# A gated mix of a long convolution and a token MLP on one core: two copies moved, an activation table loaded elsewhere, accumulating transfers reordered and re-timed in the planner

## The chip, the cores and the metric

The kernel runs on one core of a Trainium2 chip. The metric is the device time of one execution in microseconds. Before the change the median of three runs is 180.29 us (179.93 to 180.88). The profiled execution took 179.5 us; its span, from the first recorded instruction to the last, is 177.7 us, and the times below count from the start of that span. The granted TensorE clock was 1.00 all through.

A core has engines that run side by side, each through its own instruction list in order: TensorE (PE; matmuls, whose weight loads are the row PEld), VectorE (DVE), ScalarE (ACT), GpSimd (POOL) and SyncE (SP), which here issues the loads and stores. [...]

## The reference

With S = 2048 rows and D = 640 columns in bf16, and x = q:

```python
g = sigmoid((x * gate_w).sum(-1, keepdims=True))
# branch a: a 4-tap causal filter on k, times v, then a causal convolution of length S by FFT
kv = shift_filter(k, shift_k) * v
y  = irfft(rfft(pad(kv)) * rfft(pad(ssm_k)))[:S] + kv * ssm_D
a  = q * y
# branch b: layernorm over D, then an MLP over the tokens (S -> 1536 -> S)
h = layernorm(x)
u = gelu(einsum("sd,sf->df", h, w1) + b1)
b = (einsum("df,fs->ds", u, w2) + b2).T
out = g * a + (1 - g) * b
```

## The kernel before

The convolution is computed as matmuls with a table of sines (FTB), in stages. The filter ssm_k is transposed (transp, wT), transformed (fwd_c for its first half, fwd_even and fwd for its second) into C[0] and C[1], and combined across residues by additions on VectorE (mixing). k is filtered by matmuls against KF (kv), multiplied by v, transformed into C[2] (first half of the rows) and C[3] (second half), and combined in the same way. Then the spectra are multiplied on VectorE (cross, product), combined back (invmix) and transformed back by matmuls (inverse). The MLP's two products, m1 (48 groups of 8 matmuls, X with a ring of w1) and m2 (16 output tiles, GT with W2), are independent of it until the outputs are summed in O1. They have the lowest priority and fill TensorE wherever the convolution has nothing ready.

Four PSUM tiles of two banks each are shared: at most two for the MLP, at most three for the convolution. ScalarE empties nearly all of them (act), and a matmul group that finds no free tile waits.

The order of the work on each engine isn't written by hand. Every operation is given to a planner (class _Sched) with its engine, a modelled length, its reads and writes, and a priority (by default its number in the order of the program). SC.run() lets a model clock run: whenever an engine is free, the ready operation with the lowest priority value is taken. The order that comes out is then emitted, with the semaphore waits that the data need, and is fixed from there on. If the model believes a transfer to have landed sooner than it does, the instruction is emitted too early in its list and waits on the chip, with everything behind it.

What the change touches:

- **Transfers in the planner** (lines 459 to 464). All transfers share one model queue, dma_free. A transfer is due when that queue has moved it, plus 2.0 us, and plus another 6.0 if GpSimd issued it.
- **Accumulating transfers** (dma with accum=True, line 267), issued by GpSimd: they add an SBUF region into another one. Four of them form the second half of the filter's spectrum (v1mix, line 1058), two are in mixing_acc (line 1112) for C[3], four in cross (line 1250), one each in the products with a late part (line 1214), four in acc_dma (line 1227), which add the cross terms V1 into A1, and four in inverse for the first half of the output. In mixing_acc the sum and difference of lines 1113 and 1114 need both transfers of line 1112.
- **Key turns** (k_turn, line 760): VectorE reorders a block of k (kn) into kp, then SyncE issues a transposing transfer into KT. Blocks 0 and 1 have priority 0, so they go where the planner believes their data to be there.
- **Row statistics** (stats_of and ln_tile): VectorE computes mean and variance of the 16 row tiles of X in groups of 8, 5 and 3; GpSimd forms the inverse deviation (ln_scale); VectorE applies it (ln_apply). The operations are chained by `after` into one order, statistics of the next group ahead of the applies of the last.
- **Gelu** (line 1138): the first one comes when the first m1 tile is done. The activation table that it needs is loaded by an instruction that stands right ahead of it in ScalarE's list.

An `after` edge in the planner is an order of starts only; it places an operation in the emitted list and adds no wait for data.

Of the kernel before, what the change touches and what calls it, by code (L numbers as in the profile page):

```python
# [328 lines left out]
class _Sched:  # L329
# [59 lines left out]
    def run(self):  # L389
        ops = self.ops  # L390
        for op in ops:
            op.succ = []
            op.asucc = []
            op.ndep = len(op.deps) + len(op.after)
        for op in ops:
            for d in op.deps:
                d.succ.append(op)
            for d in op.after:
                d.asucc.append(op)
        engs = list(ENGS) + ["SP", "QA"]  # L400
        ready = {e: [] for e in engs}
        pend = {e: [] for e in engs}
        free = {"ACT": 2.93, "DVE": 0.85, "POOL": 0.83, "PE": 1.18, "SP": 0.0, "QA": 0.0}
        port = {"DVE": 0.0, "POOL": 0.0}
        dma_free = 0.3
        avail = {}
        for op in ops:
            avail[op] = 0.0
            if op.ndep == 0:
                heapq.heappush(pend[op.eng], (0.0, op.prio, op.idx))  # L410
        nfree = list(range(self.NSLOT))
        held = {}
        events = []
        order = []
        t = 0.0
        done = 0
        started = 0
        n = len(ops)
        frees = []
        while started < n:  # L420
            while frees and frees[0][0] <= t:
                _, sl, cls = heapq.heappop(frees)
                nfree.append(sl)
                held[cls] -= 1
            nxt = []
            progress = False
            for e in engs:
                while pend[e] and pend[e][0][0] <= t:
                    _, p, i = heapq.heappop(pend[e])
                    heapq.heappush(ready[e], (p, i))  # L430
                if free[e] > t:
                    nxt.append(free[e])
                    continue
                skipped = []
                pick = None
                while ready[e]:
                    p, i = heapq.heappop(ready[e])
                    op = ops[i]
                    if op.vt is not None and op.vt.slot is None:
                        c = op.vt.cls  # L440
                        if not nfree or held.get(c, 0) >= self.limit.get(c, 99):
                            skipped.append((p, i))
                            continue
                    pick = op
                    break
                for s in skipped:
                    heapq.heappush(ready[e], s)
                if pick is None:
                    if pend[e]:
                        nxt.append(pend[e][0][0])  # L450
                    continue
                op = pick
                progress = True
                started += 1
                if op.vt is not None and op.vt.slot is None:
                    op.vt.slot = nfree.pop(0)
                    held[op.vt.cls] = held.get(op.vt.cls, 0) + 1
                op.start = t
                if e in ("SP", "QA") or op.lat < 0:
                    issue = 1.2 if e == "POOL" else 0.1  # L460
                    s = max(t + issue, dma_free)
                    dma_free = s + op.dur
                    op.end = dma_free + 2.0 + (6.0 if e == "POOL" else 0.0)
                    free[e] = t + issue
                else:
                    op.end = t + op.dur
                    if op.lock:
                        op.end += max(port["POOL" if e == "DVE" else "DVE"] - t, 0.0)
                        port[e] = op.end
                    free[e] = op.end  # L470
                order.append(op)
                if op.vt is not None:
                    op.vt.left -= 1
                    if op.vt.left == 0:
                        heapq.heappush(frees, (op.end + 0.05, op.vt.slot, op.vt.cls))
                for s in op.asucc:
                    avail[s] = max(avail[s], op.start)
                    s.ndep -= 1
                    if s.ndep == 0:
                        heapq.heappush(pend[s.eng], (avail[s], s.prio, s.idx))  # L480
                for s in op.succ:
                    lat = 0.08 if s.eng == e else 0.15
                    if e == "PE" and s.eng == "PE":
                        lat = 0.0
                    avail[s] = max(avail[s], op.end + lat)
                    s.ndep -= 1
                    if s.ndep == 0:
                        heapq.heappush(pend[s.eng], (avail[s], s.prio, s.idx))
                nxt.append(free[e])
            if not progress:  # L490
                c = [x for x in nxt if x > t]
                if frees:
                    c.append(frees[0][0])
                assert c, "schedule stuck: " + str([(o.name, o.eng, o.ndep) for o in ops if not hasattr(o, "end")][:12])
                t = min(c)
        self.order = order
        self.makespan = max(o.end for o in ops)
        return order
# [16 lines left out]
def _build(nc, A_q, A_k, A_v, A_shift_k, A_ssm_k, A_ssm_D, B_x, B_w1, B_b1, B_w2, B_b2, gate_w, out):  # L515
# [10 lines left out]
    with ExitStack() as es:  # L526
# [434 lines left out]
        def ln_scale(a, b):  # L961
            n = b - a
            ts("POOL", sd[:, a:b], mv[:, a:b, 1], 1e-5, None, ALU.add, prio=0)
            o_ = tt("POOL", rstd[:, a:b], sd[:, a:b], V(cst, 1, [[0, n]]), ALU.pow, prio=0)
            o_.dur, o_.lock = 1.75, False
            tt("POOL", sd[:, a:b], sd[:, a:b], rstd[:, a:b], ALU.mult, prio=SDP)
# [15 lines left out]
        for h in range(2):  # L982
            for db in range(ND):
                transp(h, db)
            if h == 0:
                consts()
            if h in (1,):
                fwd_even(srcW(h), h, C[h], 1.0 / 1024.0, h == 1, "W")
            if h == 0:
# [5 lines left out]
            if h == 0:  # L995
                LB = [0, 8, 13, 16]
                nb = len(LB) - 1
                seq = []

                def chain(f, *a):  # L1000
                    n0 = len(SC.ops)
                    f(*a)
                    for o_ in SC.ops[n0:]:
                        if o_.eng == "DVE":
                            o_.after.update(seq[-1:])
                            seq.append(o_)

                pag = []

                def flush():  # L1010
                    while pag:
                        o_ = pag.pop(0)
                        o_.after.update(seq[-1:])
                        seq.append(o_)

                def stats_of(k):
                    for t in range(LB[k], LB[k + 1]):
                        b0, b1, ag = ln_tile(t // 4, t % 4)
                        b0.after.update(seq[-1:])
                        seq.append(b0)  # L1020
                        flush()
                        b1.after.update(seq[-1:])
                        seq.append(b1)
                        pag.append(ag)
                    ln_scale(LB[k], LB[k + 1])
                stats_of(0)
                for k in range(1, nb):
                    stats_of(k)
                    flush()
                    chain(ln_apply, LB[k - 1], LB[k])  # L1030
                chain(ln_apply, LB[nb - 1], 16)
                lnlast.append(seq[-1])
                for g0 in KFP:
                    tt("POOL", KF[:, g0:g0 + 20 // len(KFP), :, :], V(cw, 7 * g0, [[7, 20 // len(KFP)], [1, 7], [0, 32]]), V(m32, 0, [[0, 20 // len(KFP)], [0, 7], [1, 32]]), ALU.mult).after.update(kfirst[:1])
                    kfirst.append(SC.ops[-1])
                for hk in range(2):
                    k_turn(hk)
                mixing(C[0], SS, 0, fine=True, prio=MIXP)
            else:
                mixing(C[1], C[0], 0, conj=True, prio=MIXP)  # L1040
# [283 lines left out]
        lastp = []  # L1324
        chained(product, A1[1], A1[1], V0[1], tmp_of(q_hi, 0), V1[1])
        chained(product, A1[0], A1[0], V0[0], tmp_of(q_hi, 1), V1[0])
        acc_dma(A1[1], V1[1])
        acc_dma(A1[0], V1[0])
        chained(product, A0[1], A0[1], V0[1], H(V0[1], 0))
        lastacc = SC.ops[-1]  # L1330
        assert lastacc.eng == "POOL"
        for kt in range(2):
            dma(q_hi[:, kt, :, :], dr(A_q, 512 * kt * D, [[4 * D, 128], [1, 4 * D]]), 128 * 5120, wait=[H(A0[1], 1)]).deps.add(lastacc)
# [45 lines left out]
```

## Time and profile before

| Engine | busy us | share of the 177.7 us span |
|---|---|---|
| TensorE | 172.6 | 97% |
| TensorE weight loads | 129.4 | 73% |
| VectorE | 169.7 | 96% |
| ScalarE | 117.0 | 66% |
| GpSimd | 43.6 | 25% |

The share of time in which an engine is busy is an average over the stages. A busy TensorE row says little by itself, since matmuls overlap and their ends are modelled; the number of matmuls in a stretch, times the time of one, tells whether it runs without a break. The transfers' two large queues moved 32.16 MB (those of SyncE) and 11.14 MB (those of GpSimd, the accumulating ones). The table of transfers in the profile gives the time from issue to landing, of which waiting behind other transfers is a part.

### The profile page before, as it was taken

The page shows a single profiled execution, that of the slowest core. Times are in us where ns is not written, and L with a number is a line of the kernel's source. Part 1 is how long each engine was busy: PE and PEld are TensorE (multiplying, and loading weights), DVE is VectorE, ACT ScalarE, POOL GpSimd, SP SyncE. Part 2 cuts the span into 40 slices and gives each one's busy share as a digit, 9 for nine tenths or more (in the row PEclk, how much of TensorE's full clock was granted, in tenths as well). Part 3 has the DMA queues.
Part 4 walks back from the last instruction along what each step waited for, and adds up shares of the span by engine and source line. Part 5 has one row for each costly group of instructions (what it writes and reads, how often), then busy time and mean ns, then how long its engine had stood idle before and what let it go on. Part 6 is the DMA issues. An engine that isn't in the chain of part 4 may idle for free.

```text
span 177.7 us, 3342 instructions
## 1 busy us (share of the span) xinstructions
PE 172.6 (97%) x1380; PEld 129.4 (73%) x1381; DVE 169.7 (96%) x203; ACT 117.0 (66%) x176; POOL 43.6 (25%) x52
## 2 busy tenths in 40 slices
PE   7999999799999999999999999999999999999993
PEld 2666787487788776777777778888888887777772
DVE  7899789989999999999999999999999999999974
ACT  4999997998999999529999911231321323754760
POOL 8089803300000065000241101204343000252000
PEclk9999999999999999999999999999999999999999
DMA  4999999999999999999999998898999999499363
GB/s 136 394 411 374 391 312 156 248 414 374 191 240 315 109 216 226 231 228 278 230 227 271 205 248 299 144 225 230 188 193 217 207 218 408 167 197 212 93 241 131
DMA packets 38542, 43.51 MB, mean 245 GB/s; under 512 B 15867, under 2 KB 31360, under 8 KB 38528
## 3 DMA queue, kind: packets, MB, share of 16 engines
q1 hardware_dynamic: 33296, 32.16, 61.2%
q0 software_dynamic: 5200, 11.14, 36.5%
q8 instruction: 11, 0.18, 0.5%
q14 instruction: 3, 0.02, 0.0%
q10 hardware_dynamic: 32, 0.01, 0.0%
HBM read 25.87 MB, written 2.62 MB: 160 GB/s over the span
## 4 chain that ended last, share of the span: by engine, by line
PE 88%; DMA 5%; ACT 3%; SPq 2%; issue 0%; DVE 0%
PE pp L298 88%; DMA rows<-in_B_b_dram 5%; SPq L272 2%; ACT C L676 1%; ACT L676 1%; ACT GT L676 0%; DVE O L688 0%
## 5 line engine op out<-in xcount | busy, mean ns | idle before, releaser
L298 PE MATMUL pp<-X,ring 128*128 128x320 bf16 x384 | 55.3, 299 | 0.0
L632 DVE TENSOR_TENSOR C<-C 128x2560 bf16<-128x2560 bf16 (+2 forms) x37 | 54.5, 1523 | 0.8 <-ACT C L676 0.6
L298 PE MATMUL pp<-GT,W 128*128 128x320 bf16 x384 | 52.6, 299 | 0.0
L298 PEld LDWEIGHTS pp<-GT,W 128*128 128x128 bf16 x384 | 43.5, 113 | 8.7
L298 PEld LDWEIGHTS pp<-X,ring 128*128 128x128 bf16 x384 | 37.3, 98 | 14.3
L676 ACT ACTIVATE C<-pp 128x640 bf16<-128x640 f32 x64 | 40.7, 731 | 2.8 <-PE pp L298 2.7
L676 ACT ACTIVATE O<-pp,c,omg 128x640 bf16<-128x640 f32 x15 | 13.3, 885 | 34.7 <-PE pp L298 34.7
L267 POOL DMA_DIRECT2D C<-C x8 | 11.0, 1616 | 43.9 <-DVE C L632 43.9
L298 PE MATMUL pp<-wT,FTB 128*128 128x320 bf16 x112 | 17.1, 299 | 0.7 <-ACT GT L676 0.5
L676 ACT ACTIVATE cgb<-pp,gg 128x640 bf16<-128x640 f32 x16 | 12.7, 795 | 5.6 <-PE pp L298 5.2
L676 ACT ACTIVATE GT<-pp,cc 128x640 bf16<-128x640 f32 x12 | 9.6, 803 | 9.3 <-PE pp L298 9.2
L298 PEld LDWEIGHTS pp<-wT,FTB 128*128 128x128 bf16 x112 | 10.5, 98 | 5.6 <-ACT GT L676 0.8
L632 DVE TENSOR_TENSOR tm<-C,C 128x2560 bf16<-128x2560 bf16 (+1 forms) x7 | 14.3, 2059 | 0.0
L954 DVE BATCH_NORM_STATS2 stats<-X 128x6 f32<-128x320 bf16 x32 | 13.6, 464 | 0.5 <-DMA X<-in_A_q_dram 0.5
L298 PE MATMUL pp<-C,FTB 128*128 128x320 bf16 x96 | 13.4, 299 | 0.0
L267 POOL DMA_DIRECT2D C<-q_hi x6 | 5.9, 977 | 27.6 <-DVE C L632 12.9
L298 PEld LDWEIGHTS pp<-C,FTB 128*128 128x128 bf16 x96 | 9.4, 98 | 3.6
L676 ACT ACTIVATE gq<-gq 128x640 bf16<-128x640 bf16 x16 | 11.8, 745 | 0.2 <-DVE gq L632 0.2
L632 DVE TENSOR_TENSOR SS<-C 128x2560 bf16<-128x2560 bf16 x8 | 11.7, 1488 | 0.1
L632 DVE TENSOR_TENSOR C<-tm 128x2560 bf16<-128x2560 bf16 (+1 forms) x9 | 10.7, 1194 | 0.1
L676 ACT ACTIVATE ksh<-pp 128x1024 bf16<-128x1024 f32 (+1 forms) x12 | 9.9, 903 | 0.2 <-PE pp L298 0.2
L267 POOL DMA_DIRECT2D O<-q_hi x4 | 4.8, 1200 | 21.3 <-DVE q_hi L632 21.3
(77 smaller groups left out, 197.0 us busy)
## 6 DMA issues: line engine op xcount, KB each, us to landing
ring<-in_B_w_dram SPq DMA_DIRECT2D x12, 512.0 KB, 12.2
W<-in_B_w_dram SPq DMA_DIRECT2D x12, 512.0 KB, 5.5
C<-C POOLq DMA_DIRECT2D x8, 640.0 KB, 11.5
X<-in_A_q_dram SPq DMA_DIRECT2D x4, 640.0 KB, 8.4
kn<-in_A_k_dram SPq DMA_DIRECT2D x4, 640.0 KB, 9.4
out_dram<-O SPq DMA_DIRECT2D x7, 320.0 KB, 3.4
C<-SS POOLq DMA_DIRECT2D x3, 640.0 KB, 11.9
ssm<-in_A_ssm_k_dram SPq DMA_DIRECT2D x3, 512.0 KB, 6.8
```

Source lines behind the costliest of these rows:

```text
L267: ins = engobj.dma_start(out_ap, in_ap, accum_op=ALU.add, max_dma_last_dim=2560)
L272: ins = engobj.dma_start(out_ap, in_ap)
L298: ins = self.nc.tensor.matmul(ps_ap, lhsT=lhsT, rhs=rhs, start=start, stop=stop, skip_group_check=True)
L632: o_ = SC.add(eng, d, lambda s: T.op(eng, lambda e: e.tensor_tensor(o, a, b, op), rd, [o]), rd, [o], prio=prio, name="tt")
L676: return T.op("ACT", lambda e: e.activation(o, src, func, **kw), rr + [src], ww)
L954: ops.append(SC.add("DVE", 0.38, (lambda o, i: lambda s: T.op("DVE", lambda e: e.bn_stats(o, i), [i], [o]))(o, i), [i], [o]))
```

## The change

Three edits to the order, and one to the planner's model:

1. The two key turns of the first half get an `after` edge to the second statistics instruction of tiles 13 and 15, so they stand between the statistics of the last group.
2. A gelu of one column is put on ScalarE behind the last transposed block of the filter's second half, so that the table is loaded there. Its output, gws, is overwritten later by its real value.
3. The four accumulating transfers of acc_dma for A1 get an `after` edge to the one that belongs to the product A0[1], which so stands ahead of them in GpSimd's list. The query reload that frees q_hi for the outputs waits for that one.
4. In the planner, accumulating transfers leave the shared queue and get one of their own: 0.6 us after their issue, one after the other, 2.2 times their modelled length each, with nothing added. The other transfers are no longer held up by them in the model.

```diff
+        acc_free = 0.0
...
-                    s = max(t + issue, dma_free)
-                    dma_free = s + op.dur
-                    op.end = dma_free + 2.0 + (6.0 if e == "POOL" else 0.0)
+                    if e == "POOL":
+                        acc_free = max(t + issue + 0.6, acc_free) + 2.2 * op.dur
+                        op.end = acc_free
+                    else:
+                        s = max(t + issue, dma_free)
+                        dma_free = s + op.dur
+                        op.end = dma_free + 2.0
...
             if h == 0:
                 consts()
+            else:
+                g_ = act(gws[:, :], cst[:, 1:2], ACT.Gelu_apprx_tanh, name="tab", prio=SC.ops[-1].idx)
+                g_.dur = 1.5
+                g_.after.add(SC.ops[-2])
...
+                kpos = []
...
                         pag.append(ag)
+                        if t in (13, 15):
+                            kpos.append(b1)
...
                     k_turn(hk)
+                    SC.ops[-2].after.add(kpos[hk])
...
+        n_acc = len(SC.ops)
         acc_dma(A1[1], V1[1])
         acc_dma(A1[0], V1[0])
         chained(product, A0[1], A0[1], V0[1], H(V0[1], 0))
         lastacc = SC.ops[-1]
+        for o_ in SC.ops[n_acc:]:
+            if o_.eng == "POOL" and o_ is not lastacc:
+                o_.after.add(lastacc)
```

## The prediction

> **What bounds the kernel now.** I read the busy shares first, then the chain of work that ended last, then the timelines of TensorE and VectorE around the places that the diff names, and last the accumulating transfers one by one.
>
> ```profile
> PE 172.6 (97%) x1380; PEld 129.4 (73%) x1381; DVE 169.7 (96%) x203; ACT 117.0 (66%) x176; POOL 43.6 (25%) x52
> ```
>
> Two engines are nearly full. The chain says which of them sets the end:
>
> ```profile
> 31.60 1.28 ACT L676
> 32.89 0.01 issue
> 32.90 0.79 ACT GT L676
> 33.69 1.20 ACT C L676 x2
> 34.89 0.14 issue
> 35.02 139.97 PE pp L298 x1128
> 174.99 0.03 issue
> 175.02 0.55 DVE O L688
> ```
>
> The columns are start, length, work. From 35.02 us to 174.99 us TensorE never lets go. It is also at its pace: 8 matmuls of 320 columns take 1.09 us in the timeline, 0.136 us each; the 968 of them after 35 us make 131.6 us, and the 160 short ones of the causal filter (3.94 us for 72, 0.055 us each) 8.8 us, in sum 140.4 against the 139.97 seen. So no edit can shorten that stretch; it can only start earlier or be interrupted. The start is held up here (TensorE timeline, with the idle time ahead of each piece in brackets):
>
> ```profile
> 33.75 0.45 PE L298 MATMUL pp<-wT,FTB 128*128 128x320 bf16 x2 [0.51 <-ACT GT L676]
> 34.34 0.45 PE L298 MATMUL pp<-wT,FTB 128*128 128x320 bf16 x2 [0.15 <-ACT C L676]
> 35.02 3.94 PE L298 MATMUL pp<-KF,KT 128*128 128x128 bf16 x72 [0.24 <-ACT C L676]
> ```
>
> 0.51 + 0.15 + 0.24 = **0.90 us** is all that the gelu table load at 31.60 costs TensorE: its four PSUM tiles wait for ScalarE.
>
> VectorE has no such reserve either. Its timeline, at the lines that matter:
>
> ```profile
> 22.68 0.83 DVE L764 COPY kp<-kn 128x2560 bf16<-128x2560 bf16 x1 [1.05 <-DMA kn<-in_A_k_dram]
> ...
> 86.79 1.49 DVE L632 TENSOR_TENSOR C<-C 128x2560 bf16<-128x2560 bf16 x1
> ...
> 93.54 1.49 DVE L632 TENSOR_TENSOR tm<-C,C 128x2560 bf16<-128x2560 bf16 x1
> 94.94 0.82 DVE L632 TENSOR_TENSOR q_hi<-C,C 128x1280 bf16<-128x1280 bf16 x1
> ...
> 101.19 2.89 DVE L632 TENSOR_TENSOR C<-C 128x2560 bf16<-128x2560 bf16 x2
> ```
>
> The pair at 101.19 is the sum and difference of mixing_acc (lines 1113 and 1114). They need both accumulating transfers of line 1112, the second of which is issued at 88.83, right behind the operation at 86.79. The list of transfers in the half microsecond from 88.5 gives its time to landing (last column):
>
> ```profile
> C<-C POOLq DMA_DIRECT2D x1, 640.0 KB, 10.7
> ```
>
> It lands at 88.83 + 10.7 = 99.5, 1.7 us before its use.
>
> [...] The trace has 1.28 us, and the gelu starts 1.30 us after the load did[...]. [...] No accumulating transfer here is so short: alone in the queue 5.7 and 5.8 us (issued at 112.19 and 122.25), beside loads 7.2 and 10.7. [...] from 92 to 94 us only the hardware queue's packets appear (94.9% of 16 engines), while the transfer issued at 88.83 lies waiting.
>
> **The change, part by part.**
>
> *Gelu table.* The load is moved behind the last transposed filter block (ScalarE done at 27.78; then idle 0.88 us to 28.66 and 0.33 to 30.29). Load 1.28 plus a one-column gelu, by the nearest row (a 16-column tanh) 0.19 us: 1.47 us, of which 1.21 us lies in these idle times; the rest delays evacuations whose tiles have a free PSUM slot. Bounds of the gain: 0.90 if all of the gap goes, 0.64 if the 0.26 us left over comes through. I take 0.75.
>
> *Key turns.* They move behind the statistics of tiles 13 and 15. VectorE then does all eight applies (from 19.39, about 2.95 us) and tile 13 (0.85 us), so the first turn runs at about 23.2, after its data came at 22.68: the wait of 1.05 us is gone. The first transpose is issued 0.4 us later (23.95 for 23.53), and as it holds the queue 4.37 us, the second lands near 34.3 instead of 33.9. The filter's matmuls want it at 35.02 - 0.75 = 34.3: level, cost 0 to 0.3. VectorE gains 1.05 us, hidden behind TensorE by itself.
>
> *Planner's transfers.* This is the part with consequences. The order on every engine comes from the planner's due times (lines 459 to 464). A transfer's length there is 128 x 5120 bytes at 365 bytes/ns = 1.8 us. Before, an accumulating one was due max(issue + 1.2, shared queue) + 1.8 + 8; from 88.35, where VectorE had ended the operation at 86.79, that is 99.4 plus the loads queued ahead, and the pair stands at 101.19. After, it is due max(issue + 1.8, the accumulation before it) + 2.2 x 1.8. The first, from 84.66, is due 84.66 + 1.8 + 3.95 = 90.4; the second max(90.15, 90.4) + 3.95 = **94.4**. The pair has lower indices than the cross products, so it takes VectorE's next turn after that, 94.94, six microseconds earlier in the order. The transfer itself doesn't come earlier. VectorE runs in order: behind the waiting pair stand the cross products and the gate's gth and gpre, for which ScalarE's tanh waits in its own queue ahead of a gelu. Bounds of the wait: if the transfer takes its 10.7 us again, less the 6.1 us between 88.83 and 94.94, **4.6 us**. If it follows the first one's landing (84.90 + 7.2 = 92.1) at the slowest step I see between two landings later on (144.1 to 149.1, 5.0 us), it lands at 97.1: 2.2 us. The same loads of W2, which wait for the same matmuls, lie beside it, so I take a value nearer the long end: 3.8.
>
> What of it reaches TensorE? The inverse transform starts at 148.73 on a block that VectorE finished at 147.96 (six operations of 1.40 from 140.87 to 149.3, the fifth is the one needed): 0.77 us of slack. With the 1.05 gained at the key turn the chain can be 1.82 us late against the old clock. After that TensorE stands, because its order was laid out for a VectorE without the wait. Against the time before: 3.8 - 1.82 = **+2.0 us**.
>
> *Cross sums first in the accumulating queue.* The transfer issued at 131.21 no longer queues behind two others (9.9 us to landing); alone it takes 5.8, so lands near 137. VectorE uses it only near 143.6 and the query reload behind it has 2.7 us of reserve (landed 149.5, used 152.22): gain 0. The other four follow it, at 4.2 us each (five landed between 128.05 and 149.1): 137 + 16.8 = 153.8 instead of 149.1, while VectorE asks for them from 152.95. Shifted together, 0 to 1 us of wait, mostly taken by the planner's choice of the other block; I take 0.
>
> Sum: 180.3 + 2.0 = **182.3 us**; the 0.75 of TensorE's start is inside the wait, since VectorE sets the end of that stretch.
>
> **Rivals.** *The gap closes and nothing else happens*: the second transfer lands by 95 or the pair is not moved up. For it: alone in the queue such transfers take 5.7 to 5.8 us, just what the new due time says (1.8 + 3.95), and VectorE has 1.05 us more. Against: the four W2 loads. Time: 180.3 - 0.75 = 179.5; with the full gap 179.4. *The gain is eaten, no new wait of size*: the key transposes at 34.3 to 34.6, the late table load's 0.26, or a wait of 2.2 us at the pair, which leaves 2.2 - 1.82 = +0.4. Time 180.0 to 180.7, say 180.3. *Both waits add up*: 4.6 - 1.82 = 2.8 and 1.0 at the last sums: 184.1; I count it with the forecast.
>
> **Numbers.** Forecast (slower by a wait on the accumulating queue) 0.56, gap closed 0.30, eaten 0.14. Predicted 182.3. The range must hold the gap closed, so it starts at 179.2 (the full 0.90 and 0.2 of spread) and ends at 184.1. Faster by over 0.5% (under 179.4) needs the whole gap: 0.24. Within 0.5%: the rest of that case and the eaten one, 0.19. Slower: 0.57.
>
> **What would show it.** Right: a VectorE wait of 2 us or more for a transfer C<-C ahead of a pair C<-C near 94 us, the second of line 1112 still 9 us or more to landing, and TensorE idle around 148 us ahead of the matmuls of C and FTB. Table: the load near 27.8 us and no idle TensorE between 33 and 35. Key: no wait ahead of the first kp copy. Wrong: if the second transfer lands within 6.5 us of its issue, if the pair stays behind the cross products, or if TensorE still runs unbroken from 34.3 on; then the time is the 179.5 of the first rival.

## The result, and the profile after

The changed kernel takes 186.09 us (median of four runs, 185.75 to 187.59) where the kernel before takes 180.45 beside it: a ratio of 1.033, with a 95% interval of 1.0266 to 1.0394. The forecast of 182.3 had the direction and the place, and less than half of the size; the time lies above the range.

The median grew by 5.6 us. The two profiled runs lie further apart: that of the changed kernel is the longest of its four (187.59 us), that of the kernel before (179.5 us) is shorter than any of the four beside it, so the spans differ by 8.1 us. What follows accounts for these 8.1 us. The busy shares of the changed kernel's page:

```profile
PE 174.9 (94%) x1380; PEld 130.4 (70%) x1381; DVE 169.4 (91%) x203; ACT 116.8 (63%) x177; POOL 42.3 (23%) x52
```

VectorE's work is the same, 169.4 for 169.7 us, in a longer span: waits were added, not work. TensorE's busy time rose by 2.3 us at the same number of matmuls; the reason follows below. The chain of work that ended last has changed hands, in its shares by engine:

```profile
PE 45%; DVE 32%; DMA 11%; ACT 5%; issue 3%; SPq 2%; DVEq 0%
```

Before, TensorE alone held 88% of it. Its pieces in order of time show where it now runs (start, length, work):

```profile
86.14 2.16 ACT gq L681 x6
88.29 0.41 issue
88.70 11.50 DMA C<-C
100.30 1.49 DVE C L637
...
150.22 2.90 DVE C L637 x2
153.26 29.83 PE pp L298 x200
183.11 0.55 DVE O L693
```

An 11.5 us transfer stands in the chain, then some 50 us, mostly of VectorE, and only then TensorE. The VectorE timeline at that transfer (the change shifts line numbers by five: 637 was 632):

```profile
86.65 1.50 DVE L637 TENSOR_TENSOR C<-C 128x2560 bf16<-128x2560 bf16 x1
...
93.20 1.50 DVE L637 TENSOR_TENSOR tm<-C,C 128x2560 bf16<-128x2560 bf16 x1
100.30 1.49 DVE L637 TENSOR_TENSOR C<-C 128x2560 bf16<-128x2560 bf16 x1 [5.60 <-DMA C<-C]
101.71 0.17 DVE L637 TENSOR_TENSOR gth<-sd,gacc 128x16 f32<-128x16 f32 x1
```

The sum of mixing_acc now stands right behind the operation at 93.20, as worked out, and waits 5.60 us. In TensorE's timeline the wait comes out here; first the kernel before, then the changed one:

```profile
105.27 43.63 PE L298 MATMUL pp<-GT,W 128*128 128x320 bf16 x320
148.73 8.86 PE L298 MATMUL pp<-C,FTB 128*128 128x320 bf16 x64
...
171.55 3.42 PE L298 MATMUL pp<-GT,W 128*128 128x320 bf16 x24
```

```profile
105.76 42.54 PE L298 MATMUL pp<-GT,W 128*128 128x320 bf16 x312
153.26 11.34 PE L298 MATMUL pp<-C,FTB 128*128 128x320 bf16 x64 [4.96 <-DVE C L637]
164.43 5.60 PE L298 MATMUL pp<-GT,W 128*128 128x320 bf16 x40
169.87 4.51 PE L298 MATMUL pp<-C,FTB 128*128 128x320 bf16 x32
174.21 4.51 PE L298 MATMUL pp<-SS,FTB 128*128 128x320 bf16 x32
178.56 4.51 PE L298 MATMUL pp<-GT,W 128*128 128x320 bf16 x32
```

Three things can be read off against the kernel before. The inverse transform starts at 153.26 instead of 148.73: 4.53 us. Its 64 matmuls take 11.34 us instead of 8.86: 2.48 us. And the MLP put 312 matmuls ahead of it instead of 320, so that 32 instead of 24 are left for the end: 8 more, 1.09 us. Together 8.10 us, which is the whole difference of the two spans. The third is a loss only because TensorE stands idle ahead of the inverse: the same order costs nothing where it doesn't (e3_pair_late below). The 2.48 us have their reason in TensorE's clock; the windows around the gap (stretch and its length; busy time and, in brackets, instructions of PE, PEld, DVE, ACT and POOL; then the granted clock, the DMA share and GB/s):

```profile
148.00:153.00 5.00, 0.30 (x3) 0.00 (x0) 4.96 (x4) 0.89 (x1) 0.00 (x0) 0.85 1.05 298
153.00:155.00 2.00, 1.74 (x7) 1.02 (x8) 1.97 (x3) 0.00 (x0) 0.00 (x0) 0.50 1.07 282
155.00:157.00 2.00, 2.00 (x10) 1.08 (x8) 2.00 (x2) 0.79 (x1) 0.00 (x0) 0.50 1.09 206
157.00:159.00 2.00, 2.00 (x11) 1.21 (x10) 1.84 (x2) 0.79 (x1) 0.00 (x0) 0.66 1.12 221
159.00:161.00 2.00, 2.00 (x17) 1.47 (x15) 0.82 (x1) 1.51 (x2) 0.00 (x0) 1.00 0.85 296
```

From 153 to 157 us the clock is 0.50, and 10 matmuls are in flight in 2 us where 17 are at full clock.

The early part of the change did what it was for:

```profile
28.11 1.28 ACT L681 ACT_TABLE_LOAD   x1
29.40 0.20 ACT L681 ACTIVATE gws<-cst 128x1 f32<-128x1 f32 x1
29.51 1.28 ACT L681 ACTIVATE C<-pp 128x640 bf16<-128x640 f32 x2
31.41 0.79 ACT L681 ACTIVATE GT<-pp,cc 128x640 bf16<-128x640 f32 x1 [0.62 <-PE pp L298]
```

The load begins where ScalarE had been idle, and TensorE has no idle time between 33 and 35 us any more. But a new wait of 1.28 us, on the product vkv (the filtered k times v of the first half), has come up at 50.30.

### The profile page after: what moved, and what is told of

Its sections match the earlier page's. It is cut to its first block, busy times and chain, and to the rows that moved or that the text cites. A ratio compares the mean times of both kernels' runs of the same rounds, so it can differ in the third digit from the quotient of the medians.

```text
span 185.8 us, 3344 instructions
## 1 busy us (share of the span) xinstructions
PE 174.9 (94%) x1380; PEld 130.4 (70%) x1381; DVE 169.4 (91%) x203; ACT 116.8 (63%) x177; POOL 42.3 (23%) x52
## 4 chain that ended last, share of the span: by engine, by line
PE 45%; DVE 32%; DMA 11%; ACT 5%; issue 3%; SPq 2%; DVEq 0%
PE pp L298 45%; DVE C L637 16%; DVE tm L637 9%; DMA C<-C 6%; DMA rows<-in_B_b_dram 5%; ACT C L681 3%; DVE q_hi L637 3%; SPq L272 2%; DVE SS L637 2%; DVE vkv L637 2%; ACT gq L681 2%; DVE kp L769 0%; DVE O L693 0%; DVE c L637 0%; DVE gpre L637 0%
## 5 line engine op out<-in xcount | busy, mean ns | idle before, releaser
L681 ACT ACTIVATE C<-pp 128x640 bf16<-128x640 f32 x64 | 40.2, 736 | 2.0 <-PE pp L298 2.0
L267 POOL DMA_DIRECT2D C<-C x8 | 10.5, 1871 | 45.8 <-DVE C L637 43.0
L298 PE MATMUL pp<-C,FTB 128*128 128x320 bf16 x96 | 15.8, 333 | 5.0 <-DVE C L637 5.0
L298 PEld LDWEIGHTS pp<-C,FTB 128*128 128x128 bf16 x96 | 10.3, 108 | 10.4 <-issue 5.2
L298 PEld LDWEIGHTS pp<-wT,FTB 128*128 128x128 bf16 x112 | 10.7, 98 | 4.5 <-ACT C L681 0.2
L637 DVE TENSOR_TENSOR C<-tm 128x2560 bf16<-128x2560 bf16 (+1 forms) x9 | 10.7, 1194 | 0.1
```

The costliest lines, as they stand in the source:

```text
L267: ins = engobj.dma_start(out_ap, in_ap, accum_op=ALU.add, max_dma_last_dim=2560)
L298: ins = self.nc.tensor.matmul(ps_ap, lhsT=lhsT, rhs=rhs, start=start, stop=stop, skip_group_check=True)
L637: o_ = SC.add(eng, d, lambda s: T.op(eng, lambda e: e.tensor_tensor(o, a, b, op), rd, [o]), rd, [o], prio=prio, name="tt")
L681: return T.op("ACT", lambda e: e.activation(o, src, func, **kw), rr + [src], ww)
```

## The experiments

Theory 1: the new due times of the accumulating transfers cost it all, through the place of mixing_acc's sum and difference. Theory 2: one of the other edits does, the order of the accumulations first of all. Each ratio is to runs of the kernel before on the same chip (medians 179.7 to 179.9 us), so times of different experiments are best compared by their ratios.

**e1_old_due**: the changed kernel, with the planner's due times as before.

```diff
-                    if e == "POOL":
-                        acc_free = max(t + issue + 0.6, acc_free) + 2.2 * op.dur
-                        op.end = acc_free
...
+                    op.end = dma_free + 2.0 + (6.0 if e == "POOL" else 0.0)
```

> The changed kernel with the planner's old due times for accumulating transfers; table load, key turns and order of the accumulations stay. Theory 1 (the new due time alone costs): no wait of VectorE for C<-C near 94 us, TensorE unbroken, 179.3 to 180.6 us. Theory 2 (one of the other three edits costs, for example the accumulations of A1 landing too late): 183 us or more, with a wait near the last sums.

180.89 us, ratio 1.0065 (1.0045 to 1.0086), a little above what theory 1 had. No wait for C<-C near 94 us, so four fifths of the loss go with the due times. What is left is a loss as well: VectorE waits 1.70 us for C<-C at 154.80, TensorE 0.89 us at 164.26 and 1.55 us for vkv at 50.15. The three edits without the fourth gain nothing.

**e2_due_only**: the kernel before with the new due times alone (the first two pieces of the diff ahead of the prediction, down to `op.end = dma_free + 2.0`).

> The kernel before with nothing but the planner's new due times. Theory 1: the pair of mixing_acc moves up, VectorE waits 5 us or more for its transfer, TensorE idles about 4 to 5 us ahead of the inverse transform, 184.5 to 187 us. Theory 2: under 181.5 us, since the new due times alone harm nothing.

189.88 us, ratio 1.0562 (1.0522 to 1.0603): worse than the whole change and than expected. Theory 1 holds, and there is a second wait that I had not expected:

```profile
99.75 1.49 DVE L637 TENSOR_TENSOR C<-C 128x2560 bf16<-128x2560 bf16 x1 [4.66 <-DMA C<-C]
...
151.63 5.82 DVE L637 TENSOR_TENSOR C<-C 128x2560 bf16<-128x2560 bf16 x4 [3.03 <-DMA C<-SS]
```

The second is for the transfer of the product A0[1], 15.7 us from issue to landing behind two others. Edit 3 puts that transfer ahead of others: in the changed kernel it takes 6.0 us and nobody waits for it.

**e3_pair_late**: the changed kernel, with the pair of mixing_acc put behind the third cross product, where it had stood. TensorE's and SyncE's orders stay those of the changed kernel.

```diff
+                if n_ == 2:
+                    for p_ in pair:
+                        p_.after.add(o_)
```

> The changed kernel with the pair of mixing_acc placed behind the third cross product, where it stood before; TensorE's order is that of the changed kernel to the last instruction. Theory 1, narrow (of all that the new due times move, the place of this pair is what costs): no wait for C<-C, 179.8 to 181.5 us (the 1.28 us for which TensorE waits on vkv near 50 us may remain). Theory 1, wide (other moves by the new due times cost too): 182 to 184 us. Theory 2: 184 us or more.

179.73 us, ratio 0.9991 (0.9972 to 1.001). The pair doesn't wait, though its transfer takes 11.2 us:

```profile
100.60 2.89 DVE L637 TENSOR_TENSOR C<-C 128x2560 bf16<-128x2560 bf16 x2
```

TensorE runs from 49.57 to 174.9 without a break. The narrow form of theory 1 is confirmed: the place of these two instructions (the two that need them follow) is the whole loss. The new due times are kept here, and so is edit 3; the wait at 154.80 that e1_old_due had is absent. Ahead of the pair the order is the changed kernel's, and yet TensorE waits only 0.19 us for vkv: that wait differs from profile to profile (see the key turns further on).

**e5_hold_w2**: the changed kernel, with the first load of W2, and so all of them, held until the second transfer of mixing_acc has landed. The orders of all engines are those of the changed kernel.

```diff
+                hold = [V(C[3], SL, [[1, SL]])] if (n_, a) == (0, 0) else []
...
+                if hold:
+                    w2last.deps.add(macc[1])
```

> The changed kernel with every load of W2 held back until the second transfer of mixing_acc has landed; all engine orders are those of the changed kernel. If the loads are what makes the transfer late: it lands 6 to 7.5 us after its issue, VectorE waits under 1.5 us instead of 5.6, 180 to 182.5 us (the first W2 tiles must still come before 105 us). If an accumulating transfer behind another one is that slow by itself: 10 us or more to landing, a wait of 4.5 us or more, 185 to 188 us.

180.75 us, ratio 1.0057 (1.0038 to 1.0076). The list of transfers issued from 88.3 to 89.3 us gives the time to landing (last column), first in the changed kernel, with the loads beside it, then in this one:

```profile
C<-C POOLq DMA_DIRECT2D x1, 640.0 KB, 11.5
```

```profile
C<-C POOLq DMA_DIRECT2D x1, 640.0 KB, 5.7
```

and VectorE passes the pair without a stop:

```profile
93.11 1.49 DVE L637 TENSOR_TENSOR tm<-C,C 128x2560 bf16<-128x2560 bf16 x1
94.51 1.49 DVE L637 TENSOR_TENSOR C<-C 128x2560 bf16<-128x2560 bf16 x1
```

So the transfer is late because of the W2 loads, and the new due time (5.75 us after the issue, or 3.95 us after the one ahead) is right for a transfer that has no loads beside it (5.7 us measured). The remaining 1.0 us of loss isn't settled. In the profile TensorE waits 1.46 us for vkv at 50.20 and, ahead of the inverse, 0.45 and 0.15 us at 148.65 and 150.05; VectorE, with the gate's operations now behind the pair, waits 1.10 us for ScalarE at 100.11.

**e4_table_only**: the kernel before with the early table load.

```diff
+                g_ = act(gws[:, :], cst[:, 1:2], ACT.Gelu_apprx_tanh, name="tab", prio=SC.ops[-1].idx)
+                g_.dur = 1.5
+                g_.after.add(SC.ops[-2])
```

> The kernel before with the early gelu table load alone. Theory (the prediction's step): the load lies near 28 us, TensorE idles under 0.3 us between 33 and 35 us instead of 0.90, and the time falls by 0.4 to 0.9 us. Rival: the planner's new order opens another gap (as the wait on vkv near 50 us in the changed kernel, 1.28 us) that takes the gain back: within 0.3 us of before or above.

180.4 us, ratio 1.003 (1.0013 to 1.0047): the rival came true. The gap at 33 us is gone; in the order that the planner then makes TensorE idles 0.59 us at 43.56, 0.22 at 50.36 and 0.42 at 148.53.

**e7_key_only**: the kernel before with the two key turns behind tiles 13 and 15 (`SC.ops[-2].after.add(kpos[hk])`).

> The kernel before with the key turns' places alone. Theory: the wait ahead of the first kp copy (1.05 us) is gone, but the next loads of k sit in SyncE's list behind the two transposes, so VectorE waits for them near 40 us instead (1 to 1.6 us, before 0.21), and the time is that of before within 0.3 us. Rival: VectorE keeps its 1.05 us and the time falls by 0.3 us or more.

179.77 us, ratio 0.9995 (0.9981 to 1.001): no change, as the theory had it. The wait ahead of the first copy is gone; another of 0.76 us stands ahead of the third, for the loads of k behind the transposes (1 to 1.6 us were expected), and a wait of 0.83 us for ScalarE ahead of it.

**e8_acc_order**: the kernel before with edit 3 alone (`o_.after.add(lastacc)`). Only GpSimd's order differs.

> The kernel before with the cross sums ahead in the accumulating queue alone; every other engine's order is that of before. Theory: the last sums for A1 land 153 to 155 us instead of 149, VectorE waits 1 to 2 us for C<-C near 153 us, TensorE 0.3 to 1 us near 163 us: 0.4 to 1.2 us slower. Rival (the prediction's: taken up by slack): within 0.3 us of before.

181.21 us, ratio 1.007 (1.0047 to 1.0093). VectorE's and TensorE's timelines have

```profile
155.52 1.49 DVE L632 TENSOR_TENSOR SS<-C 128x2560 bf16<-128x2560 bf16 x1 [2.16 <-DMA C<-C]
```

```profile
164.98 4.51 PE L298 MATMUL pp<-C,FTB 128*128 128x320 bf16 x32 [1.42 <-DVE C L632]
```

The four accumulations that now come last are late for the last sums, and the plan, made with the old due times, still puts these sums where they were. With the new due times and the same edit (e3_pair_late) nobody waits for them. Edit 3 alone costs 1.3 us; it and the new due times fit each other.

**e6_spin** and **e13_spin_first** ask for the clock: the changed kernel with 23 matmuls of 512 columns that nobody reads.

```diff
-                    mms(vt, items, name="inv")
+                    lead = h == 0 and p == 2 and kt == 0
+                    m_ = mms(vt, ([((lambda s: s[:, 0:512]), V(FTB, 0, [[1, 128]]), V(FTB, 0, [[1, 512]]), True, True)] * 23 if lead else []) + items, name="inv")
+                    if lead:
+                        m_.dur = 8 * (320 / 2400.0 + 0.0025)
```

> The changed kernel with 23 added matmuls of 512 columns on the sine table ahead of the first inverse group, about 4.9 us of work that nobody reads, which lies in the 5 us in which TensorE waits there; everything else unchanged. If the idle TensorE is then given a slower clock, which costs up to 2.5 us after the wait: the clock stays at 1.00, the 64 matmuls behind the wait take 8.9 us instead of 11.3, and the time falls by 1 to 2.5 us. If the slow matmuls have another cause (the transfers beside them): no change, or the added work's overhang more.

Here lead stood for the block p == 0, which is not the first one that runs: the added matmuls came behind the first group, after the wait. 191.09 us, ratio 1.065 (1.0596 to 1.0704); the added work simply adds, so the time says nothing on the clock.

> The changed kernel with the 23 added matmuls (4.9 us at full clock, read by nobody) ahead of the first inverse group that is run, where TensorE waits 5 us; in e6_spin they came behind that group and so added 5 us. If idling is what slows the clock: granted clock 1.00 all through, the 64 inverse matmuls take 8.9 instead of 11.3 us, 1 to 2.5 us faster than the changed kernel. If not: within 0.7 us of it.

184.65 us, ratio 1.027 (1.0236 to 1.0305). The changed kernel's ratio was 1.033, so the difference is about 1.1 us; as the two intervals overlap, the time alone decides nothing, and the trace has to. TensorE's timeline (22 of the 23 matmuls are in the trace) and the windows:

```profile
147.71 4.91 PE L298 MATMUL pp<-FTB 128*128 128x512 bf16 x22
152.46 8.86 PE L298 MATMUL pp<-C,FTB 128*128 128x320 bf16 x64
```

```profile
148.00:153.00 5.00, 5.00 (x26) 2.36 (x25) 4.96 (x4) 0.59 (x1) 0.00 (x0) 1.00 1.06 304
153.00:155.00 2.00, 2.00 (x17) 1.46 (x15) 1.97 (x3) 0.96 (x2) 0.00 (x0) 1.00 1.09 210
```

VectorE still waits (4.93 us) and the inverse still starts late, at 152.46, but TensorE isn't idle, its clock stays 1.00, and the 64 matmuls take 8.86 us as in the kernel before. The orders of the other engines are the changed kernel's. So it was the idling that slowed the clock here: 0.50 with 4.96 us of idle time, 1.00 with none.

**e11_table_order** and **e12_table0_key** look for a better kernel: the early load with `g_.dur = 0.01`, so that the planner's order stays what it was, alone and with the key turns.

> The kernel before with the early table load, which the planner is told costs nothing (0.01 us), so that the order of TensorE, VectorE and SyncE is that of before to the last instruction and ScalarE's only differs by the load's place. Theory (the load's place is worth the gap, and what e4_table_only lost came from the new order): TensorE idles under 0.3 us between 33 and 35 us, nothing new opens later, 0.4 to 0.9 us faster than before. Rival (start and VectorE set the rest, so closing the gap moves the wait elsewhere): within 0.3 us of before.

> The kernel before with the key turns' places and the early table load at no cost in the planner; otherwise the order of e7_key_only. Theory: VectorE's 1.05 us from the key turn gives the earlier TensorE the room that it needs near 149 and 163 us, 0.5 to 1.0 us faster than before. Rival: the wait for k near 40 us keeps VectorE where it was, no more than e11_table_order gives.

179.62 us, ratio 0.9987 (0.997 to 1.0004), and 179.68 us, ratio 0.9976 (0.9956 to 0.9996). The gap at 33 us is closed in both, and each shows TensorE waits of 0.2 to 0.5 us near 50 us instead. Neither has the gain that its theory had (0.4 to 0.9 and 0.5 to 1.0 us). The second is the only version here whose interval lies below 1, by 0.04 to 0.44%. Its ratio stands for 0.4 us, but its median is only 0.06 us below that of the kernel before (179.74), and one interval of eleven that just misses 1 is weak evidence: if there is a gain, it is less than the 0.75 us at which the table alone was priced.

## Why the prediction was right or wrong

**What bounds the kernel** was right, and so was the point that no edit could gain more than TensorE's 0.90 us of gaps. No version gained even that.

**The mechanism** was right: the place behind the operation at 93.5 that the due time of 94.4 called for, the wait for C<-C, the idle TensorE ahead of the inverse. e3_pair_late shows that it is all of the loss, and e5_hold_w2 that the W2 loads make the transfer late.

**The step that failed is the sum "3.8 - 1.82 = +2.0"**: its wait was too short and its room too large, and it had no term for what the idle time then does to TensorE.

**The wait was mis-sized.** I bounded it by 2.2 and 4.6 and took 3.8. It was 5.60 in the profiled run (4.66 to 5.76 in the experiments that have it). The long end was taken for a limit because the transfer had taken 10.7 us once; it took 11.5 this time. The short end supposed that it would go on right after the first one landed, though the windows that I had quoted showed the hardware queue alone at work from 92 to 94 us. A single measured time in a contended stretch is no bound; with the loads beside it, the transfer took 10.7 us in the kernel before, 10.8 in e2_due_only, 11.2 in e3_pair_late and 11.5 in the changed kernel and in e1_old_due.

**VectorE's 1.05 us at the key turn** was counted as room, and in the profiled run it was not there. VectorE was 0.14 us ahead of before at 86 us and 0.34 at the operation ahead of the pair (93.20 for 93.54). The saving reappears as a wait at the third key copy, here before and after:

```profile
39.94 0.83 DVE L764 COPY kp<-kn 128x2560 bf16<-128x2560 bf16 x1 [0.21 <-DMA kn<-in_A_k_dram]
```

```profile
40.06 0.83 DVE L769 COPY kp<-kn 128x2560 bf16<-128x2560 bf16 x1 [1.32 <-DMA kn<-in_A_k_dram]
```

The next loads of k stand in SyncE's list behind the two transposes (8.2 us of issue), and so go out no earlier for VectorE's being early:

```profile
33.05 1.20 SPq L272 DMA_DIRECT2D kn<-in_A_k_dram  x2
```

```profile
33.24 1.20 SPq L272 DMA_DIRECT2D kn<-in_A_k_dram  x2
```

I named that queue for TensorE's sake and did not follow it to the loads behind it. e7_key_only agrees. How much room is left is a matter of the profile: in e3_pair_late and e13_spin_first, with the same order up to there, the third key copy ran at 39.32 and 39.22 instead of 40.06, and VectorE was 1.06 and 1.13 us ahead at the same operation (92.48 and 92.41); in the first of them the transposes held SyncE for 7.1 us instead of 8.2; TensorE's wait for vkv near 50 us was then 0.19 us and none. Why the transposes took less isn't known.

**Left out of the sum** were two terms. The slower clock after the idle time cost 2.48 us in the profiled run, and about 1.1 us by the ratios (e13_spin_first). TensorE stood idle for 4.96 us. The clock was 1.00 until 151.5, 3.2 us after TensorE stopped, 0.53 from there to 152, 0.50 to 158, and 1.00 again from 158.4, 5.1 us into its work. The idle time that I forecast, 2.0 us and 2.8 at the long end, is shorter than these 3.2 us, and idle times of 1.28 us (the changed kernel), 1.46 (e5_hold_w2) and 1.55 (e1_old_due) near 50 us left it at full speed: 1.00 in the first one's windows there, a mean of 0.999 and 1.00 in the other two runs. No profile quoted here has an idle time in between, so it is my estimate that this term came in with the mis-sized wait; I had asked for no price of a longer one. The other term: the new order has one group of 8 MLP matmuls behind the inverse that had been ahead of it, 1.09 us that could have filled a part of the idle time.

With the measured terms the sum works for the profiled run: 5.60 of wait, less 0.77 of slack and 0.34 of lead, is 4.49, seen as 4.53; plus 2.48 plus 1.09. The median's loss of 5.6 us is smaller, as the experiments with shorter waits and the higher mean clock of two of the other runs would have it, but the runs behind it weren't profiled.

**The gelu table**: the place and the 1.47 us were right (1.28 + 0.20), and so was the closed gap. The 0.75 us of gain was wrong even alone: e4_table_only is slower by 0.3%, because the planner's order changed with it, and where the order was held (e11_table_order) the time didn't differ measurably. Why no more comes of a gap of 0.90 us isn't settled: TensorE's early wait for a bias load, 0 to 0.8 us from profile to profile, is as large as the gain, and small waits near 50 us took part of it.

**The cross sums first**: the 6.0 us to landing were right (I had 5.8). The wait that I set to 0 within 0 to 1 is 2.16 us in the old plan (e8_acc_order) and 0 in the changed kernel, whose late VectorE asks later. That this edit removes a wait which edit 4 makes (3.03 us of VectorE in e2_due_only) I had not seen; I judged it against the plan before, where nothing waited. By the ratios of e2_due_only and the change (1.0562 and 1.033 of 180 us) edits 1 to 3 together are worth 4 us in the new plan; no run has edit 3 with the new due times alone, so its own share isn't shown.

## What to carry to other kernels

A planner's due time is a claim on the chip: before changing it, look for the first instruction that it moves up, and compare its new place with the measured landing of what it waits for, in the traffic of that stretch and not in an empty queue (here 11.5 us beside the loads, 5.7 without). The idle TensorE was paid for twice here: 4.53 us of late start, and 2.48 us at a clock of 0.50. So price a predicted gap of several microseconds a second time, through the clock (it slowed in the gap of 4.96 us and not in those of 1.28 to 1.55). A wait that disappears gains nothing until one has followed the engine to its next wait.

## What the runs showed of the hardware that I had not expected

The same 640 KB accumulating transfer, issued at the same place, took 5.7 us from issue to landing with no load beside it (e5_hold_w2) and 10.7 to 11.5 us beside the 512 KB loads of W2, of which three (kernel before) or four (changed kernel) are issued from 84 to 95 us. In the kernel before, the accumulation ahead of it had landed at 92.1, yet from 92 to 94 us the loads' queue alone shows packets (packets, MB, share of the 16 DMA engines):

```profile
q1 hardware_dynamic: 596, 0.59, 94.9%
```

From 94 to 95 us the accumulating queue has 5.3%, from 95 to 96 us 78.9%. Why it shows so few packets in these 3 us, the trace doesn't tell.

The price of an idle TensorE differed from run to run. In the profiled run of the changed kernel (4.96 us idle) the clock was near one half for 6.8 us, as read from the granted clock in narrow windows. In e6_spin (5.11 us idle) it was 0.68, 0.50 and 0.97 in the three windows of 2 us from 152 to 158 us, which at a clock of 0.50 makes 3.4 us. For the rest there is an estimate from mean clock and span, with 0.50 for the slow clock: 6.7 us in the profiled run of e2_due_only (5.90 us idle; 0.982 in 187.4 us), and 7 us for two of the changed kernel's four runs and 3.5 us for the others (0.981 twice, 0.990 and 0.991).
